# TensorE's share of a side computation moved ahead of half loads and scores in each step of an attention kernel

## The chip, the cores and the metric

The kernel runs on one core of a Trainium2 chip. The metric is the device time of one execution in microseconds (us); the time of a kernel is the median of its runs. Five engines with queues of their own take part: TensorE (PE; its weight loads are listed apart as PEld), VectorE (DVE), ScalarE (ACT), GpSimd (POOL) and SyncE (SP, which only issues DMAs).

## The reference

Two blocks follow one another. The first is attention over 8 batches, 8 heads, 576 tokens and 64 dimensions a head, in which each query keeps the 32 keys with the highest scores:

```python
scores = scale * np.matmul(q, k.transpose(0, 1, 3, 2))
kth = np.partition(scores, -top_k, axis=-1)[..., -top_k:-top_k + 1]
scores = np.where(scores >= kth, scores, -1e9)
attn = softmax(scores)          # exp of scores less their maximum, over their sum
x = np.matmul(attn, v)          # heads side by side: 576 x 512 a batch
```

The second is a mixture of depths: a gate for each token (`x @ w_gate`), and for the 128 tokens of a batch with the highest gates a two-layer network, whose result is weighted by the sigmoid of the gate and added to the row. The other rows pass through.

```python
h = np.maximum(xe @ w1, 0.0)    # 128 x 1024
out[b, top_idx] = x[b, top_idx] + g[:, None] * (h @ w2)
```

## The kernel before

**Units.** The attention is cut into 144 units of 128 query rows by two heads: 18 a batch (`per_batch`), in the order batch, tile of rows `t`, pair of heads `g`. The last tile has 64 rows and holds four heads a unit. One loop, `for n in range(-1, N)`, is a software pipeline written out by hand. Program order is kept on every engine (the class `InOrder`, whose line 45 is therefore the line of nearly every instruction in the profile), so the order of the statements is the order of each engine's queue.

**One step.** In step `n` the statements do, in this order:

- `weigh` for unit `n - 4`: TensorE turns the unit's scores (`ptr<-ident,sc`, `av<-ident,sc` for the last block) and adds a large negative number where the mask `less` says that the key isn't among the 32 (`ptr<-out_of_reach,less`). The first eight blocks need the mask's first half, the next eight its second half. Then ScalarE takes the exponentials (`pT` of the two times four blocks, `last` of the last).
- `mask_of` for unit `n - 3`: `less`, the first half by ScalarE, the second by GpSimd (by VectorE in the steps of `scatter_steps`); both need VectorE's `next`.
- `flush()`: what lies in the list `late` goes to ScalarE (the ReLU of the mixture, its copies).
- TensorE turns one or two blocks of the next batch's keys and queries into free columns of the scores' PSUM (half loads, `ps<-ident,rows`), then multiplies the scores of unit `n + 1` (`ps<-kT,qT`). ScalarE copies both out (`kT`, `qT`, `sc`).
- `values` for unit `n - 4` on TensorE: weights times values (`av<-v,pT`, 32 products, and `av<-vpair,last`, four for the last keys). It needs `pT` and `last`. ScalarE copies the result (`xs`) and, at the end of a tile, its sums (`sums`).
- VectorE: `bound_of` for unit `n` (the maxima `cand`, `best`, `bound`), between its halves what lies in `vector_late` (reciprocals `rden`, the gates' products `prod`, the mixture's counts `junk`); then `kth_of` for unit `n - 2` (`next<-y`). `flush_pool()` gives GpSimd what lies in `pool_late`.
- `what_is_below` for unit `n - 1`: ScalarE's `sides<-sc,bound`, GpSimd's `y<-sc,sides` and its short fill `y<-steps,seen`.
- the mixture's piece for step `n`, if there is one.

At the end of a batch `keep_least` adds VectorE's `low` and three reductions.

**The mixture.** `mixture` is a generator. `mix_steps` lists for each step which batch's generator is advanced by one `yield`, once or several times; the pieces of batch `b` stand in the steps of batches `b + 1` and `b + 2` (`mix_at`; a denser list for the last two mixtures, `mix_at_of`). The pieces are: the gate row through DRAM (three DMAs on SP), five counts for VectorE, the places (five small products on TensorE, advanced inside the step by `place_steps`, not by `mix_steps`), a gather of 128 rows, their four transposes (`xe_ps`), eight pieces of four products for the first layer (`h_ps`, one ReLU for every two of them) and eight of one product of 512 columns for the second (`y_ps`; the profile counts two matmuls for each). The results of TensorE's pieces lie in one PSUM bank with a single buffer (`misc`). What other engines do for a piece is put into `late`, `vector_late` or `pool_late` and goes out at the next flush.

PSUM is the reason for the tight order: the scores, the turned scores, the values and the mixture have one buffer each (`ps_sc`, `ps_tr`, `ps_av`, `ps_misc`).

Behind the loop the last units are finished statement by statement (from line 1214), and `closing` does the last batch's mixture.

Of the kernel before, what the change touches and what calls it, by code (L numbers as in the profile page):

```python
# [48 lines left out]
def kernel(  # L49
# [118 lines left out]
    def load_weights():  # L168
        sp.dma_start(
            out=wg, in_=dataclasses.replace(moe_w_gate, ap=[[0, P], [1, HD]])  # L170
        )
        sp.dma_start(out=w1, in_=moe_w1.rearrange("(c p) f -> p c f", p=P))
        sp.dma_start(out=w2, in_=moe_w2.rearrange("(c p) n -> p c n", p=P))
# [13 lines left out]
    def flush():  # L187
        while late:
            late.pop(0)()
# [15 lines left out]
    def room_for_qkv(b):  # L205

        kT = kqpool.tile([P, NHP, R + S], FP32, name="kT")  # L210
        qT = kqpool.tile([P, NHP, S], FP32, name="qT")
        return kT, qT, vbufs[b % 2]
# [98 lines left out]
    def turn_pair(rows, hp, copy=None):  # L311
        tr = ps_tr.tile([P, 2, J, P], FP32, name="ptr")
        for w in range(2):
            rows.turn(2 * hp + w, tr[:, w, :, :])
        for w in range(2):
            rows.keep(2 * hp + w, tr[:, w, :, :], copy=copy)
# [8 lines left out]
    def load_v(vb, vs):  # L325
        vt, vpair = vs
        v_rows = vb[:, JP:S, :].rearrange("h p d -> p h d")
        for hh in range(2):
            sp.dma_start(
                out=vpair[hh * R : (hh + 1) * R, :, hh, 0:D], in_=v_rows[:, hh::2, :]  # L330
            )
        for h in range(H):
            sp.dma_start(
                out=vt[:, h, :, 0:D],
                in_=vb[h, 0:JP, :].rearrange("(p j) d -> p j d", j=J),
            )

    def groups(t):

        return NHP // 2 if t == J else NHP  # L340
# [11 lines left out]
    def room_for_scores():  # L352
        return ps_sc.tile([P, 2, 2, 512], FP32, name="ps")

    def multiply(t, g, kT, qT, ps):

        n = R if t == J else P  # L360
        for u in range(2):
            for i, heads in enumerate(heads_of(t, g)):
                at = u * HALF + (0 if i else R)
                d = slice(i * D, (i + 1) * D)
                for h, r in heads:
                    pe.matmul(
                        ps[r : r + n, i, u, 0:HALF],
                        qT[d, h // 2, t * P : t * P + n],
                        kT[d, h // 2, at : at + HALF],
                    )  # L370
# [106 lines left out]
    def room_to_turn():  # L477
        return ps_tr.tile([P, 2, J, P], FP32, name="ptr"), ps_av.tile(
            [P, 512], FP32, name="av"
        )  # L480
# [62 lines left out]
    def normalise(b, t, xs):  # L543
        n = R if t == J else P
        den = sums[0:n, b * NT + t, :]
        divide(n, xs, of_batch[b][0][0:n, t, :], den)

    def keep_sums(n, xs, den):
        act.activation(den, xs[0:n, :, D], AF.Copy, bias=1e-9)
# [404 lines left out]
    def gates(b, t):  # L954
        dot_tile(t, *of_batch[b])
# [24 lines left out]
    N = len(units)  # L980
# [16 lines left out]
    mix_steps = {}  # L997
# [9 lines left out]
    for b in range(B - 1):  # L1007
        n = (b + 1) * per_batch + mix_at_of.get(b, mix_at)[6]
        mix_steps[n].remove(b)
        place_steps[n] = b  # L1010
    mixtures = {}
# [21 lines left out]
    def is_unit(n):  # L1033
        return 0 <= n < N

    def weigh(sc, tr, av, less):

        turn(sc, tr, less)
        tr_last = turn_last(sc, av, less)
        pT = ptpool.tile([P, 2, J, P], FP32, name="pT")  # L1040
        last = ptpool.tile([P, P], FP32, name="last")

        def exp():
            act.activation(pT, tr, AF.Exp, scale=scale)
            act.activation(last, tr_last, AF.Exp, scale=scale)

        return pT, last, exp
# [25 lines left out]
    def keep_least(b, bound, kth):  # L1073
        low = stats.tile([P, per_batch, 2], I32, name="low", bufs=1)
        dve.tensor_scalar(
            out=low,
            in0=bound.bitcast(I32),
            scalar1=(1 << 23) - 1,
            scalar2=1,
            op0=ALU.bitwise_and,  # L1080
            op1=ALU.bitwise_xor,
        )
        for w, of in enumerate((bound, kth, low)):
            dve.tensor_reduce(
                out=least[:, w, b : b + 1], in_=of, axis=mybir.AxisListType.XY, op=ALU.min
            )

    def mask_of(n, on=None):
        b, i = divmod(n, per_batch)
        masks[n] = mask(scs[n], next8s[b][:, i, :, :], on)  # L1090
        if i == per_batch - 1 and b < B - 1:
            keep_least(b, bounds.pop(b)[:, :, :, 7], next8s.pop(b)[:, :, :, 7])

    for n in range(-1, N):
        b, i = divmod(n, per_batch)
        if i == 0 and 0 <= b < B - 1:
            qkv[b + 1] = room_for_qkv(b + 1)
            loading = chain(
                loading, Rows(k[b + 1], q[b + 1], *qkv[b + 1][0:2]).parts()
            )  # L1100
        if 0 < n + 1 < NHP:
            turn_pair(first_rows, n + 1)
        if n == 1:
            load_v(v[0], qkv[0][2])
        if n == NHP:
            load_weights()


        gating = normalised
        if inverting is not None:  # L1110
            normalised = inverting[0:2]
            vector_late.insert(0, lambda a=inverting: normalise(*a))
            inverting = None
        else:
            normalised = None
        if gating is not None:
            vector_late.append(lambda a=gating: gates(*a))

        if is_unit(n - 4):
            tr, av = room_to_turn()
            pT, last, exp = weigh(scs.pop(n - 4), tr, av, masks.pop(n - 4))
            exp()
        if is_unit(n - 3):
            mask_of(n - 3, (act, None) if n in scatter_steps else None)
        flush()
        if is_unit(n + 1):
            b, t, g = units[n + 1]
            ps = room_for_scores()  # L1130
            kT, qT = qkv[b][0:2]
            b, i = divmod(n, per_batch)
            loads = list(islice(loading, first_loads[i] if b == 0 else loads_at[i]))
            halves = [ps[:, a, :, HALF : HALF + P] for a in range(2)]
            for load, half in zip(loads, halves):
                load[0](half)
            multiply(t, g, kT, qT, ps)
            for load, half in zip(loads, halves):
                load[1](half)
            scs[n + 1] = keep(ps, n == -1)  # L1140
        if is_unit(n - 4):
            b4, t4, g4 = units[n - 4]
            values(t4, g4, pT, last, av, qkv[b4][2])
            if n in place_steps:
                values_bank[0] = av
                next(mixtures[place_steps[n]])
            if g4 == 0:
                xs = xpool.tile([P, H, DE], FP32, name="xs")
                if t4 == 0:
                    x = xpool.tile([P, NT, HD], FP32, name="x")  # L1150
                    pg = gates_of[b4 % 2]
                    of_batch[b4] = x, pg
            keep_values(t4, g4, av, xs)
            if g4 == groups(t4) - 1:
                inverting = b4, t4, xs
                n4 = R if t4 == J else P
                keep_sums(n4, xs, sums[0:n4, b4 * NT + t4, :])
            while kept:
                kept.pop(0)()


        if is_unit(n):
            bound_of(n)
        flush_vector()
        flush_pool()
        if is_unit(n - 2):
            kth_of(n - 2)
        while after_kth:
            after_kth.pop(0)()


        if is_unit(n - 1):
            what_is_below(n - 1)

        if gating is not None:
            b, t = gating
            if t == J:
                store(out[b], of_batch[b][0])
                mixtures[b] = mixture(float(b * S), of_batch[b][1], ranks[:, b, :])
        for b in mix_steps.get(n, ()):  # L1180
            next(mixtures[b], None)
        b, i = divmod(n, per_batch)
        if i == v_at and 0 <= b < B - 1:
            load_v(v[b + 1], qkv[b + 1][2])
# [12 lines left out]
    def weigh_unit(m):  # L1197
        tr, av = other_room() if (N - m) % 2 else room_to_turn()
        weighed[m] = *weigh(scs.pop(m), tr, av, masks.pop(m)), av
# [10 lines left out]
    def sums_of(t, xs):  # L1210
        n = R if t == J else P
        keep_sums(n, xs, sums[0:n, (B - 1) * NT + t, :])

    weigh_unit(N - 4)
    weighed[N - 4][2]()
    what_is_below(N - 1)
# [188 lines left out]
```

## Time and profile before

| | |
|---|---|
| median of 3 runs | 827.2 us (826.03 to 827.62) |
| profiled execution | 828.44 us |
| its span in the profile | 826.1 us |
| instructions | 28252 |
| mean granted TensorE clock | 0.99 of full speed |
| HBM read, written | 36.93 MB, 11.55 MB |

The profile has one row for each group of instructions with the same engine, operation and tiles: busy time, mean duration, and the idle time of the engine ahead of them with what ended most of it. Its slices show the busy share in tenths in 40 equal parts of the span. The windows give the same per stretch; the waits sum up who waited for whom; the timeline lists instructions by start and duration, neighbours of one kind merged. The chain that ended last tells little here, for it consists of the last scatter alone. Matmuls are pipelined and their ends are modelled, so on TensorE distances between starts are the safer measure; a VectorE instruction is likewise shown starting some 0.08 us before the one ahead of it ends.

### The profile page before, as it was taken

Reading aid. Unit: us, or ns where it says so; the run is one execution under the profiler, and the core shown is the slowest. Engines: PE = TensorE matmul, PEld = TensorE weight load, DVE = VectorE, ACT = ScalarE, POOL = GpSimd, SP = SyncE. Lnnn points to the kernel's source line nnn. Section 1 sums busy time; section 2 is a strip of 40 time slices with the busy share of each in tenths; the row PEclk is TensorE's granted clock in tenths of the full one; section 3 lists DMA queues with packets and bytes.
Section 4 is the critical chain, followed back from the end, with each engine's and each line's share of the span. In section 5 each row is a group of like instructions: output and inputs, shape, how many; then the busy total and the mean of one; then the engine's idle time right before and its main releaser. Section 6 shows DMA issues by size and latency. Waiting matters only on the chain. (4 is left out here: it accounts for less than half of the span.)

```text
span 826.1 us, 28252 instructions
## 1 busy us (share of the span) xinstructions
PE 777.0 (94%) x10143; PEld 596.5 (72%) x10143; DVE 787.2 (95%) x4651; ACT 730.7 (88%) x1557; POOL 715.4 (87%) x722
## 2 busy tenths in 40 slices
PE   6888888888999999999999999999999999999976
PEld 5566666666887778877787777877787777767744
DVE  7899999999999999999999999999999999999960
ACT  4799999999999999999999999999999999879831
POOL 3799999999899999999899999999999998899831
PEclk9699999999999999999999999999999999999999
DMA  7931111521141221521223221512215102101021
GB/s 170 283 86 40 28 66 28 105 53 27 60 92 36 53 40 59 112 47 34 79 47 86 53 40 60 104 23 54 40 59 112 28 15 66 23 12 18 2 71 30
DMA packets 122133, 50.38 MB, mean 61 GB/s; under 512 B 116417, under 2 KB 116417, under 8 KB 120961
## 3 DMA queue, kind: packets, MB, share of 16 engines
q1 hardware_dynamic: 118672, 43.91, 22.0%
q0 software_dynamic: 1728, 4.20, 2.8%
q8 instruction: 82, 1.34, 0.8%
q14 instruction: 67, 0.54, 0.3%
q10 hardware_dynamic: 1584, 0.39, 0.2%
HBM read 36.93 MB, written 11.55 MB: 59 GB/s over the span
## 5 line engine op out<-in xcount | busy, mean ns | idle before, releaser
L45 POOL TENSOR_TENSOR y<-sc,sides 128x576 f32<-128x576 f32 x288 | 365.1, 1289 | 57.0 <-ACT sides L45 54.3
L45 DVE MAX8 cand<-sc 128x8 f32<-128x82 f32 (+1 forms) x2016 | 314.0, 228 | 2.7 <-ACT sc L45 2.7
L45 POOL TENSOR_SCALAR less<-sc,next 128x576 bf16<-128x576 f32 x135 | 232.5, 1722 | 12.9 <-DVE next L45 10.0
L45 PE MATMUL ptr<-out_of_reach,less 128*128 128x128 bf16 x1136 | 205.3, 220 | 19.5 <-POOL less L45 19.4
L45 ACT ACTIVATE sides<-sc,bound 128x576 bf16<-128x576 f32 x288 | 223.0, 787 | 0.0
L45 PE MATMUL ptr<-ident,sc 128*128 128x128 f32 x1136 | 217.0, 282 | 0.0
L45 DVE MAX8 next<-y 128x8 f32<-128x584 f32 x288 | 204.4, 751 | 1.7 <-POOL y L45 1.6
L45 PEld LDWEIGHTS av<-v,pT 128*64 128x64 f32 x4544 | 144.1, 137 | 66.9 <-ACT last L45 63.2
L45 PE MATMUL ps<-kT,qT 64*128 64x288 f32 (+1 forms) x1280 | 182.0, 431 | 5.2 <-ACT qT L45 5.2
L45 PEld LDWEIGHTS ptr<-ident,sc 128*128 128x128 f32 x1136 | 161.3, 142 | 29.1 <-issue 17.4
L45 ACT ACTIVATE pT<-ptr 128x1024 f32<-128x1024 f32 x142 | 145.3, 1023 | 33.2 <-PE ptr L45 32.2
L45 PE MATMUL av<-v,pT 128*64 128x65 f32 x4544 | 163.7, 224 | 9.3 <-ACT last L45 8.5
L45 ACT COPY sc<-ps 128x1152 f32<-128x1152 f32 (+1 forms) x144 | 162.2, 1126 | 3.5 <-PE ps L45 3.5
L45 PEld LDWEIGHTS <-less 128*128 128x128 bf16 x1296 | 136.1, 106 | 39.2 <-POOL less L45 25.2
L45 PEld LDWEIGHTS ps<-kT,qT 64*128 64x128 f32 (+1 forms) x1280 | 100.2, 178 | 41.5 <-issue 21.2
L45 ACT ACTIVATE less<-sc,next 128x576 bf16<-128x576 f32 x143 | 111.2, 777 | 12.7 <-DVE next L45 10.8
L45 DVE MATCH_REPLACE8 cand<-best,cand 128x21 f32<-128x21 f32 (+1 forms) x576 | 99.0, 180 | 0.0
L45 DVE MAX8 best<-cand 128x8 f32<-128x21 f32 (+1 forms) x576 | 90.5, 190 | 0.0
L45 PE MATMUL h_ps<-xeT,w 128*128 128x128 f32 x464 | 65.8, 286 | 0.0
L45 PEld LDWEIGHTS h_ps<-xeT,w 128*128 128x128 f32 x464 | 55.8, 191 | 9.2 <-issue 5.8
L45 PE MATMUL y_ps<-w,hT 128*128 128x512 f32 x112 | 60.6, 636 | 0.0
L45 ACT ACTIVATION_READ_ACCUMULATOR sides<-sc,bound 128x1 f32 x288 | 59.9, 208 | 0.0
(133 smaller groups left out, 866.4 us busy)
## 6 DMA issues: line engine op xcount, KB each, us to landing
v<-in_v_dram SPq DMA_DIRECT2D x64, 128.0 KB, 4.2
out_dram<-x SPq DMA_DIRECT2D x8, 1024.0 KB, 3.9
rows<-in_k_dram SPq DMA_DIRECT2D x56, 128.0 KB, 2.9
rows<-in_q_dram SPq DMA_DIRECT2D x56, 128.0 KB, 3.1
w<-in_moe_w_dram SPq DMA_DIRECT2D x2, 2048.0 KB
gate_row<-row_dram SPq DMA_DIRECT2D x7, 288.0 KB, 4.4
w<-in_k_dram SPq DMA_DIRECT2D x8, 128.0 KB, 3.2
last<-in_k_dram SPq DMA_DIRECT2D x8, 128.0 KB, 4.0
```

What stands on the lines that cost most here:

```text
L45: return lambda *a, **kw: self._tc.keep_in_program_order(fn(*a, **kw))
```

## The change

The call that advances the mixture's generators leaves the end of step `n`, where it follows `values` and everything else, and stands in step `n + 1` instead, right behind the turning and the exponentials of unit `n - 3` and ahead of the mask, the flush, the half loads and the scores. On TensorE a piece was between the products with the last keys of one step and the turning of the next; it is now between the turning and the half loads. The places, advanced by `place_steps`, stay where they were, and the pieces of the loop's last step are still issued behind the loop. The scheduled step numbers aren't changed.

```diff
+    def mix(n):
+        for b in mix_steps.get(n, ()):
+            next(mixtures[b], None)
+
     for n in range(-1, N):
...
             pT, last, exp = weigh(scs.pop(n - 4), tr, av, masks.pop(n - 4))
             exp()
+        mix(n - 1)
         if is_unit(n - 3):
             mask_of(n - 3, (act, None) if n in scatter_steps else None)
         flush()
...
                 mixtures[b] = mixture(float(b * S), of_batch[b][1], ranks[:, b, :])
-        for b in mix_steps.get(n, ()):
-            next(mixtures[b], None)
         b, i = divmod(n, per_batch)
...
+    mix(N - 1)
     weigh_unit(N - 4)
     weighed[N - 4][2]()
```

## The prediction

> **What bounds the kernel now.** I read the page first: who is busy, and when.
>
> ```profile
> PE 777.0 (94%) x10143; PEld 596.5 (72%) x10143; DVE 787.2 (95%) x4651; ACT 730.7 (88%) x1557; POOL 715.4 (87%) x722
> PE   6888888888999999999999999999999999999976
> DVE  7899999999999999999999999999999999999960
> ```
>
> Then the windows over one batch (18 steps, from the middle, where one batch repeats the last):
>
> ```profile
> core 0: us, PE busy (x) PEld busy (x) DVE busy (x) ACT busy (x) POOL busy (x), PEclk, DMA share, GB/s
> 307.00:403.10 96.10, 94.92 (x1269) 73.58 (x1266) 95.99 (x577) 91.53 (x197) 88.51 (x88) 1.00 0.27 60
> ```
>
> VectorE works 95.99 of 96.10 us: it paces the middle, at 96.1/18 = 5.34 us a step. But nobody is far behind: TensorE 94.92, ScalarE 91.5, GpSimd 88.5. The waits of the whole span say who waits for whom behind VectorE's back:
>
> ```profile
> PEld av L45 <- ACT last L45: 63.2, 132, 1.3
> POOL y L45 <- ACT sides L45: 54.3, 71, 12.0
> ACT pT L45 <- PE ptr L45: 32.2, 75, 1.6
> PEld L45 <- POOL less L45: 25.2, 30, 1.4
> ```
>
> The first and third are what the change is about: TensorE idles before `values` for ScalarE's exponentials, and ScalarE idles for the turned scores. Neither is VectorE's time.
>
> Last, the timelines of one step, engine by engine:
>
> ```profile
> 417.18 0.39 PE L45 MATMUL ps<-ident,rows 128*128 128x128 f32 x2
> 418.67 1.15 PE L45 MATMUL av<-v,pT 128*64 128x65 f32 x32
> 419.65 0.39 PE L45 MATMUL av<-vpair,last 128*64 128x130 f32 x4
> 419.98 1.16 PE L45 MATMUL h_ps<-xeT,w 128*128 128x128 f32 x8
> 420.97 0.27 PE L45 MATMUL ptr<-ident,sc 128*128 128x128 f32 x1
> ...
> 420.22 0.30 ACT L45 COPY xs<-av 128x130 f32<-128x130 f32 x1
> 420.38 0.82 ACT L45 ACTIVATE sides<-sc,bound 128x576 bf16<-128x576 f32 x1
> ```
>
> ```profile
> 414.13 1.72 POOL L45 TENSOR_SCALAR less<-sc,next 128x576 bf16<-128x576 f32 x1
> 419.49 1.71 POOL L45 TENSOR_SCALAR less<-sc,next 128x576 bf16<-128x576 f32 x1
> ...
> 421.43 2.53 POOL L45 TENSOR_TENSOR y<-sc,sides 128x576 f32<-128x576 f32 x2 [0.23 <-ACT sides L45]
> 423.91 0.22 POOL L45 TENSOR_TENSOR y<-steps,seen 128x16 f32<-128x16 f32 x1
> ```
>
> TensorE's order is turn (415.64), loads and scores (417.18), values (418.67), piece (419.98), turn (420.97). The piece costs 0.99 us from its start to the next turn's.
>
> **What the edit moves.** No instruction is added or removed. The pieces number 7 transposes of `xe`, 56 of `h` (0.99 us) and 56 of `y` (0.96), less those left in the closing. Only their place on TensorE changes: turn, piece, loads and scores, values. The queues `late`, `vector_late` and `pool_late` are flushed at the same places as before, after the new call too, so ScalarE's and GpSimd's orders stay, and so do SP's DMAs (the gate row's three follow the same stores and precede the same loads). On VectorE one `squash` goes behind a gate's product in one batch: nothing. `mix(N - 1)` behind the loop is where it was. First pieces with work on TensorE stand near 203 us.
>
> Counted from before, scores and values come after the same sum of TensorE work; the turn comes 0.99 us earlier, if its mask is there. That is the point. Take the turn at 415.64. After the change it can start at 414.65, its first half takes 0.68, but the second half needs GpSimd's `less`, which ends at 414.13 + 1.72 = 415.85. So the second half starts at about 415.91 (release 0.06) instead of 416.32, and TensorE has waited 0.58 us, time that the piece filled before. From there: second half and last block 0.86 (416.32 to 417.18), piece 0.99, loads and scores 1.49, and values start at 419.25 against 418.67: 0.58 later. Their copy `xs` on ScalarE (420.22, ready then) starts at about 420.67, 0.45 later, and with it `sides` and GpSimd's `y`. The exponentials of that unit gain nothing, for ScalarE was busy until 417.2.
>
> So the piece leaves TensorE's private order and enters a loop that closes over two steps: second half of the turn 0.86, piece 0.99, loads and scores 1.49, values 1.37, to `xs` 0.05, to `sides` 0.16, to `y` 1.05, to its fill 2.48, to `less` 0.20, `less` and release 1.78. Sum 10.43. Mean extras are 0.13 (`sums` adds 0.29 in 5 of 18 steps, second copies and double loads the rest): 10.56, or 5.28 us a step. Without the piece it was (10.56 - 0.99)/2 = 4.79. VectorE needs 5.34. The slack of the loop falls from 0.55 to 0.06 us a step: GpSimd, once late, hardly catches up.
>
> **What lateness costs.** It doesn't starve VectorE at once: `y` is ready 3.7 us before `next` reads it (424.13 and 427.82). It costs where VectorE and GpSimd collide. The gate's product and `low` take longer beside a GpSimd instruction:
>
> ```profile
> 462.08 1.12 DVE L45 CUSTOM_DVE_ANT_0 prod<-x,wg 128x512 f32<-128x512 f32 x1
> ...
> 461.91 1.73 POOL L45 TENSOR_SCALAR less<-sc,next 128x576 bf16<-128x576 f32 x1
> ```
>
> Begun 0.17 behind `less`, the product took 1.12 us; begun 0.63 behind (409.38), 0.67. So it can't move in the first 0.6 us of a `less`. Behind a `y` it waits for that one's end (57.20: 1.75 us). In a middle batch five products take 4.48 us, 1.13 above 5 x 0.67, and `low` takes 1.06 against 0.17 free (at 113.15): 2.02 us of stalls. In the first batch, where `y` is ready only 1.0 us ahead (60.27, 61.28), the products alone take 8.68: 5.33 of stalls, 3.3 more. The lost slack moves the middle towards that batch. Ends: all stalls gone, -2.02 a batch; the first batch's state everywhere, +3.3. I take +1.0, a third of the way, since `y` should keep 1 to 2.5 us of its 3.7. Over (782 - 203)/96.1 = 6.0 batches that is +6.0.
>
> The Trainium skill has a rule that speaks against any such overlap: by "SBUF — State Buffer", section "Who interferes with whom", a VectorE instruction with two SBUF inputs and a GpSimd one that reads SBUF exclude each other for the whole instruction. The rows above disagree, since the product ended 0.44 us before `less` did. By the rule it would have waited 1.56, not 0.45, and five such would add 5.5 us a batch.
>
> In the double steps near 693 to 738 us (two pieces, 1.9 us) the loop takes about 0.45 more a step; VectorE waits there 1.9 us for the gate row's DMA anyway. Ends 0 and +3 over six such steps; I take +0.5. At the end two turns lie behind double pieces: ScalarE waits 1.19 and 1.61 for them (774.22, 780.29), and VectorE later 1.35 for `y` (785.33). With the turn first that could give back 1.0; a GpSimd that arrives late takes as much. Ends -1.0 and +1.5, taken as 0.
>
> Sum: +6.5. The profiled execution took 828.4 (span 826.1 and 2.3 around it), so 834.9; it lay 1.2 above the median of the three runs, 827.2. Against the median: 833.7.
>
> **Rivals.** (1) No change: VectorE paces, the loop's 0.06 us of slack suffices, the collisions stay: 827.2 within 1.7. For it: VectorE without gaps, 3.7 us of reserve. Against: the 0.45 us shown above appears at each turn whose mask ends late.
> (2) Faster: the masks are mostly there, ScalarE's wait for `ptr` (32.2) goes, `sides` and `y` come earlier, and the products start deeper into `less`. The stalls fall by a third (-0.6 x 6.0), and the end gives 1.0: 822.6. It decides at the second half of the turn: it needs `less` to end within 0.68 us of the earlier start. In the pass above it ended 1.2 after it, in the next (turn at 419.25 + 1.31 = 420.56, mask at 421.20) 0.64 after it, just in time.
> (3) The loop becomes the bound. If a pass costs 0.3 us more than my rows (releases I can't see, the piece ahead of scores costing more), a step takes 5.43, against VectorE's 5.34; 579/5.34 = 108 steps of 0.09 and rising collisions of 1 a batch give +16: 843.
> That the edit doesn't move the work is excluded: program order is kept on each engine.
>
> **How the numbers follow.** A measurement here can tell about 0.2%, 1.7 us, from no change. Slower by collisions: 0.57, its own range 829 to 839. Rival 3: 0.20. Rival 1: 0.10. Rival 2: 0.13. Faster 0.13, same 0.10, slower 0.77. The range reaches to 826 below (leaving out most of rival 2) and 843 above (leaving out under half of rival 3).
>
> **What would show it.** Right: TensorE's wait for `last` falls under 25 us; its waits for `less` (25.2 on the weight loads) rise above 50; the five products of a middle batch take over 5.0 us in place of 4.48; VectorE still has no gaps; `y` is ready under 2.6 us before its reader. Wrong: the products unchanged or shorter (rival 1 or 2), ScalarE's wait for `ptr` near zero with earlier `y` (rival 2), or VectorE idling for `sc` or `y` in the middle (rival 3).

## The result, and the profile after

The changed kernel takes 829.2 us (median of 7 runs, 828.7 to 831.6) against 826.3 us of the kernel before in the same comparison (7 runs, 825.6 to 827.6): a ratio of 1.0037, 95% interval 1.0025 to 1.0048. It is slower by about 3.0 us, as forecast in direction; the forecast of +6.5 us was more than twice too large.

The page of the changed kernel, busy times:

```profile
PE 777.8 (94%) x10143; PEld 594.7 (72%) x10143; DVE 790.1 (96%) x4651; ACT 732.6 (89%) x1557; POOL 715.3 (87%) x722
```

VectorE works 2.9 us longer than before (787.2) with the same instructions, and still has no gaps in the middle. One middle batch in the windows of the changed kernel (columns as in the prediction):

```profile
305.18:401.85 96.67, 95.45 (x1269) 73.50 (x1265) 96.56 (x577) 91.62 (x197) 88.30 (x88) 1.00 0.27 60
```

A batch takes 96.67 us in place of 96.10, with VectorE busy for all of it. The five distances from one `low` to the next, from the second to the seventh, add up to 483.53 us where they were 480.83: +2.70 of the 3.0 us. Behind the seventh `low` the profiled executions differ by 0.2 us (135.74 and 135.54), so the double steps and the end cost next to nothing, as far as one profiled execution of each can tell. (The profiled spans, 826.7 and 826.1, differ less than the medians, because the first 50 us, where the two programs are the same, took 2.3 us more in the profiled execution of before. All comparisons of profiled executions below therefore start at a `low`.)

The waits of the changed kernel:

```profile
POOL y L45 <- ACT sides L45: 60.8, 72, 11.0
PEld L45 <- POOL less L45: 33.3, 48, 1.4
PEld av L45 <- ACT last L45: 26.1, 52, 1.2
ACT pT L45 <- PE ptr L45: 7.3, 12, 1.6
```

The edit does what it says. The wait for `last` went from 63.2 to 26.1 us and ScalarE's for `ptr` from 32.2 to 7.3: 62 us of waiting gone (16.9 came back on the weight loads as a wait with ScalarE's `less`), and the kernel is slower. Most of the 63.2 was no lost time of TensorE: it is counted on the weight loads (PEld), while the matmuls of the scores still ran. The matmuls' own wait for `last` was small, before and after:

```profile
PE av L45 <- ACT last L45: 8.5, 16, 1.1
PE av L45 <- ACT last L45: 4.1, 10, 0.7
```

What grew is GpSimd's wait for `sides`, 54.3 to 60.8, and ScalarE's wait for VectorE's `next` ahead of its half of `less`. Before and after:

```profile
ACT less L45 <- DVE next L45: 10.8, 15, 2.7
ACT less L45 <- DVE next L45: 18.8, 38, 2.5
```

In one middle batch ScalarE didn't wait for `next` at all before, and waits 1.8 us in five places after: another engine now waits for VectorE.

Where VectorE spends the 0.57 us of a batch is seen in two of its five products. The timelines of the kernel before, third product and fifth, with the `less` beside each:

```profile
344.67 0.89 DVE L45 CUSTOM_DVE_ANT_0 prod<-x,wg 128x512 f32<-128x512 f32 x1
...
344.28 1.72 POOL L45 TENSOR_SCALAR less<-sc,next 128x576 bf16<-128x576 f32 x1
...
387.83 0.83 DVE L45 CUSTOM_DVE_ANT_0 prod<-x,wg 128x512 f32<-128x512 f32 x1
...
387.37 1.72 POOL L45 TENSOR_SCALAR less<-sc,next 128x576 bf16<-128x576 f32 x1
```

and the same two of the changed kernel:

```profile
342.89 1.10 DVE L45 CUSTOM_DVE_ANT_0 prod<-x,wg 128x512 f32<-128x512 f32 x1
...
342.70 1.72 POOL L45 TENSOR_SCALAR less<-sc,next 128x576 bf16<-128x576 f32 x1
...
386.25 1.16 DVE L45 CUSTOM_DVE_ANT_0 prod<-x,wg 128x512 f32<-128x512 f32 x1
...
386.12 1.72 POOL L45 TENSOR_SCALAR less<-sc,next 128x576 bf16<-128x576 f32 x1
```

Begun 0.39 us behind `less`, the third product took 0.89 us; begun 0.19 behind, 1.10. The fifth went from 0.46 behind and 0.83 to 0.13 behind and 1.16. In all four it ends 1.28 to 1.29 us after `less` began: what GpSimd starts later, VectorE waits longer. Of the 18 steps of a batch, numbered from 0, the five products stand in steps 3, 5, 9, 13 and 17; the third and the fifth are those in 9 and 17. The first, second and fourth take 0.67, 0.99 and 1.10 us before and 0.67, 1.02 and 1.11 after. The five add up to 5.05 us, against 4.48.

### The profile page after: what moved, and what is told of

Read it like the earlier page. It is cut to its first block, busy times and chain, and to the rows that moved or that the text cites. A ratio compares the mean times of both kernels' runs of the same rounds, so it can differ in the third digit from the quotient of the medians.

```text
span 826.7 us, 28221 instructions
## 1 busy us (share of the span) xinstructions
PE 777.8 (94%) x10143; PEld 594.7 (72%) x10143; DVE 790.1 (96%) x4651; ACT 732.6 (89%) x1557; POOL 715.3 (87%) x722
## 5 line engine op out<-in xcount | busy, mean ns | idle before, releaser
L45 POOL TENSOR_TENSOR y<-sc,sides 128x576 f32<-128x576 f32 x288 | 365.5, 1290 | 63.7 <-ACT sides L45 60.8
L45 PE MATMUL ptr<-ident,sc 128*128 128x128 f32 x1136 | 225.4, 287 | 0.0
L45 PEld LDWEIGHTS av<-v,pT 128*64 128x64 f32 x4544 | 144.1, 137 | 60.4 <-ACT last L45 26.1
L45 PEld LDWEIGHTS <-less 128*128 128x128 bf16 x1296 | 140.1, 109 | 35.8 <-POOL less L45 33.3
L45 DVE MAX8 best<-cand 128x8 f32<-128x21 f32 (+1 forms) x576 | 90.3, 189 | 0.0
L45 PE MATMUL h_ps<-xeT,w 128*128 128x128 f32 x464 | 63.3, 281 | 0.0
L45 PE MATMUL y_ps<-w,hT 128*128 128x512 f32 x112 | 58.5, 617 | 0.0
L45 ACT ACTIVATION_READ_ACCUMULATOR sides<-sc,bound 128x1 f32 x288 | 57.3, 199 | 0.0
```

Source lines behind the costliest of these rows:

```text
L45: return lambda *a, **kw: self._tc.keep_in_program_order(fn(*a, **kw))
```

## The experiments

My theory, A: the 3 us are VectorE's third and fifth product, which stall longer because GpSimd's `y`, and with it its next `less`, comes later. The rivals: B, the longer loop over TensorE, ScalarE and GpSimd holds the batch by itself; C, the loss lies in the double steps and the end; and later D, that loop holds the batch at about 96.0 us in both kernels, and VectorE's stalls only fill what is left.

All kernels below are timed against the kernel before. Since most of them turned out to be about which VectorE instruction stalls, here is one table for all: the time per middle batch (mean of the two between the fourth and the sixth `low`), and how much of it VectorE spends on the four kinds of instruction that take longer beside GpSimd (distances from start to start, in us). The time of everything else on VectorE is 90.3 to 90.6 us in every row, so that the four columns account for each batch. They say where VectorE's time goes; as a stalled instruction counts as busy, they don't say which engine holds the batch.

| kernel | us, ratio (95%) | batch | prod | low | less | pick |
|---|---|---|---|---|---|---|
| before | 826.3 | 96.11 | 4.15 | 0.98 | 0.42 | 0.20 |
| changed | 829.2, 1.0037 (1.0025 to 1.0048) | 96.66 | 4.71 | 0.98 | 0.42 | 0.20 |
| e1_prod_later_before | 824.8, 0.9976 (0.9965 to 0.9988) | 96.01 | 4.70 | 0.34 | 0.42 | 0.20 |
| e1_prod_later_after | 834.7, 1.0093 (1.0075 to 1.0111) | 97.41 | 4.97 | 0.37 | 1.13 | 0.60 |
| e1_five_back | 832.1, 1.0060 (1.0041 to 1.0078) | 96.93 | 4.11 | 1.03 | 1.15 | 0.30 |
| e2_late_y_before | 831.5, 1.0060 (1.0044 to 1.0076) | 96.28 | 3.57 | 1.00 | 1.14 | 0.20 |
| e2_sides_first_before | 830.6, 1.0042 (1.0026 to 1.0057) | 96.89 | 4.99 | 0.21 | 1.14 | 0.20 |
| e2_y_only | 830.3, 1.0042 (1.0029 to 1.0055) | 96.34 | 4.36 | 0.98 | 0.42 | 0.20 |
| e3_gates_later_before | 825.1, 0.9984 (0.9972 to 0.9996) | 96.08 | 3.69 | 0.69 | 1.00 | 0.36 |
| e3_gates_later_after | 829.6, 1.0032 (1.0020 to 1.0043) | 96.09 | 3.84 | 0.98 | 0.42 | 0.49 |
| e3_behind_scores_relu | 839.1, 1.0155 (1.0142 to 1.0169) | 98.42 | 5.09 | 1.18 | 1.14 | 0.43 |
| e4_half_h_before | 824.1, 0.9974 (0.9962 to 0.9985) | 95.98 | 4.01 | 0.98 | 0.42 | 0.20 |
| e4_half_h_after | 827.5, 1.0007 (0.9995 to 1.0018) | 96.22 | 4.24 | 0.99 | 0.42 | 0.20 |
| e4_half_product_before | 822.7, 0.9954 (0.9939 to 0.9969) | 96.21 | 3.91 | 0.22 | 1.13 | 0.42 |
| e4_half_product_after | 824.4, 0.9970 (0.9958 to 0.9983) | 96.12 | 3.37 | 1.03 | 0.95 | 0.41 |

Without collisions the four would take 3.0, 0.1, 0.4 and 0.2 (from the shortest rows of each kind; `prod` 1.65 in the two e4_half_product rows, where it is shorter), 3.7 in all.

**VectorE's small work later.** Between the two halves of `cand` VectorE does its products, reciprocals, counts and, in one step a batch, a half of `less`. The edit, made on both kernels:

```diff
-            if i == 1:
-                flush_vector()
             for u in range(PARTS):
+                if i == 1 and u == 4:
+                    flush_vector()
```

Expected of the changed kernel with it: 

> The changed kernel, with VectorE's small work between the halves of cand (reciprocals, gates' products, counts) moved four maxima further down its queue (about 0.59 us). Theory A (the 3 us of the change are the third and the fifth product of a batch, which begin too early into GpSimd's less): all five products begin at least 0.7 us behind the start of less and take 0.67 us, 3.35 a middle batch in place of 5.05, the batch falls from 96.67 to about 95.0 us, the whole to 817 to 821 us. Theory B (the longer loop over TensorE, ScalarE and GpSimd holds the batch at 96.67): the products get shorter but VectorE gets gaps instead, and the time stays above 827. Theory C (the 3 us lie in the double steps and the end): the time falls as much as the kernel before does with the same edit, and the 3 us between the two stay.

Expected of the kernel before with it: 

> The kernel before, with the same shift of VectorE's small work by four maxima. Theory A: products 3.35 us a middle batch in place of 4.48, batch about 95.0 in place of 96.1, the whole 817 to 821 us, within 1 us of the changed kernel with the same shift, so that the order of TensorE no longer matters. Theory B: about 820 here, and 3 us or more below the changed kernel with the shift. Theory C: 3 us below it.

Measured: 834.7 and 824.8. Theory A's numbers failed in both. The second batch shows the intended effect (three products of 0.67 us, begun 0.74 to 1.32 behind `less`), and from then on VectorE, being faster, stands differently against GpSimd: the products meet `y` or the start of `less` instead. In the changed kernel this went further: the half of `less` that VectorE makes, and `pick`, take longer too (1.13 and 0.60 us). Yet VectorE has none of the gaps in either that theory B foresaw, so B failed as well, and the difference between the two grew from 3 to 10 us, so that theory C (the loss lies in the end) is out. What follows: the collisions aren't a fixed sum that one shift removes. They depend on where VectorE stands against GpSimd, and that moves with each change.

**Five pieces put back**, in the steps just ahead of the two products:

```diff
-        mix(n - 1)
+        if (n - 1) % per_batch not in (6, 7, 13, 14, 15):
+            mix(n - 1)
...
+        if n % per_batch in (6, 7, 13, 14, 15):
+            mix(n)
```

Expected: 

> The changed kernel, with five of a batch's 17 pieces put back to the end of their step (those of positions 6, 7, 13, 14 and 15 of 18, just ahead of the third and the fifth product), the other twelve where the change has them. Theory A: the third and fifth product take 0.89 and 0.83 us again, the batch 96.1 us, the whole 826 to 827 us. Theory B (each moved piece costs its share of the loop): 12/17 of the 3 us stay, about 828.4.

Measured: 832.1 us, slower than with all of them moved. The products did fall back (4.11 us, before 4.15), but the half of `less` on VectorE grew. It is in the timelines of this kernel:

```profile
392.44 1.22 DVE L45 TENSOR_SCALAR less<-sc,next 128x576 bf16<-128x576 f32 x1
...
390.81 2.52 POOL L45 TENSOR_TENSOR y<-sc,sides 128x576 f32<-128x576 f32 x2
```

The kernel before has this instruction with no `y` beside it:

```profile
393.33 0.50 DVE L45 TENSOR_SCALAR less<-sc,next 128x576 bf16<-128x576 f32 x1
```

In this kernel a step that goes over from the moved place to the old one holds two pieces (the moved one of the step before and its own), which I hadn't thought of: twice a batch TensorE does 0.94 us more in one step, `y` comes later (3.07 us of reserve in the median, against 3.59), and other instructions are hit. Neither theory had it.

**A part without such steps**: only the pieces of positions 10 to 17 moved. Edit: in the same way, with `(n - 1) % per_batch >= 10`. Expected: 

> Only the pieces of positions 10 to 17 (the second layer in a middle batch) have the changed place, the others the old one; no step holds two. Theory A: the third product (position 9) is 0.89 us as before, the fifth (position 17) 1.16 as after; batch 96.4, 828.0 to 829 us. If every moved piece costs its share of the 3 us: 8 of 17, 828.6, with both products grown by about half.

Measured: in a middle batch the third product is 0.89, as before, the fifth 1.05 to 1.13; batch 96.34. This is theory A's picture in the profile, product by product, and not that of an equal share for every moved piece. The time, +4.0 us by the medians with an interval of +2.4 to +4.5, is above the 1.7 to 2.7 forecast; the profiled execution is 2.1 longer from the first `low` on. Theory A holds for the batch; for the rest of the time it is inconclusive.

**`y` late, TensorE untouched.** In the kernel before, ScalarE makes `xs` twice in nine steps:

```diff
             keep_values(t4, g4, av, xs)
+            if n % per_batch in (5, 7, 8, 9, 11, 13, 14, 15, 16):
+                keep_values(t4, g4, av, xs)
```

Expected: 

> The kernel before, TensorE's order untouched; ScalarE makes the copy xs a second time (0.30 us, the same data) ahead of sides in nine of a batch's 18 steps (positions 5, 7, 8, 9, 11, 13, 14, 15 and 16), those in which the change made GpSimd's y 0.2 to 0.34 us late. Theory A (what the change costs is only the phase of GpSimd against VectorE): the third and the fifth product grow to about 1.1 us each, a middle batch to 96.5 to 96.8 us, the whole to 829 to 831 us, as the changed kernel. Theory B (what costs is the longer loop over TensorE): ScalarE has 4.5 us of idle time a batch, the copies take 2.7 of it, and the time stays at 827.

Measured: 831.5, just above theory A's range of 829 to 831, and far above theory B's 827. So the kernel gets as slow with TensorE's order untouched. But the expected picture shows in one batch of five only: the batches took 97.5, 96.15, 96.42, 96.14 and 96.72, and in the last of these the third, fourth and fifth product took 1.18, 1.15 and 1.14 us. In the batches of 96.1 the dose had been too large, and a product came ahead of `less` altogether:

```profile
367.26 0.68 DVE L45 CUSTOM_DVE_ANT_0 prod<-x,wg 128x512 f32<-128x512 f32 x1
...
367.37 2.16 POOL L45 TENSOR_SCALAR less<-sc,next 128x576 bf16<-128x576 f32 x1
```

Now the product takes 0.68 us and `less` 2.16 in place of 1.72: GpSimd pays. Lateness doesn't cost in proportion: a product that begins 0.6 us behind the start of `less` pays nothing, from there on each 0.1 us nearer costs 0.1 us, up to 0.5, and one that begins first mostly pays nothing again (but 1.40 us in e1_prod_later_before at 224.47, 0.12 ahead of `less` and 0.07 behind the start of the short fill). That the second copies act through `y` alone isn't shown: they also hold up what ScalarE does next.

**`sides` ahead of `xs`** on ScalarE, so that `y` needn't wait for values:

```diff
+            if is_unit(n - 1):
+                what_is_below(n - 1)     # sides alone; y stays where it was
             keep_values(t4, g4, av, xs)
```

Expected of the kernel before with it: 

> The kernel before, with ScalarE's sides ahead of xs and sums in each step, so that GpSimd's y no longer waits for values. Theory A: less starts when next is there, the products begin 1.0 us behind it and take 0.67 each, low some 0.2 to 0.5; VectorE's batch falls by 1.2 to 1.9 us, as far as TensorE (94.9 us busy) lets it: 95.0 to 95.4 a batch, 820 to 823 us in all. Theory B: xs and av come free 1.6 us later, TensorE waits for av, and the time is above 827.

Expected of the changed kernel with it: 

> The changed kernel with the same order on ScalarE. Theory A: the late values no longer reach y, so the products are as short as in the kernel before with this edit, and the time is within 1.5 us of it, 820 to 824 us. Theory B: the change's own loop (turn, piece, scores, values) holds the batch, and the time stays 3 us or more above the kernel before with this edit.

Measured: 830.6 and 877.1 (1.0619, 1.0602 to 1.0636). Theory A failed and B was right, in both. Values' bank now comes free some 1.5 us later (two `sides`), and TensorE's turning needs it for its last block. The changed kernel's waits with this edit:

```profile
PEld av L45 <- ACT xs L45: 78.8, 126, 0.9
PE av L45 <- ACT xs L45: 49.0, 115, 0.7
```

With the piece behind the turning there is no other work on TensorE that could cover this wait; in the kernel before the piece stands ahead of the turning and covers most of it (27.6 and 17.5 us of the same two waits there). A batch of the changed kernel takes 105.6 us here and VectorE has gaps: this is what a loop over TensorE looks like when it does become the bound, and the changed kernel alone shows none of it.

**The piece behind the scores.** First with its ReLU in the next step, as the kernel has it:

```diff
-        mix(n - 1)
...
             scs[n + 1] = keep(ps, n == -1)
+        mix(n - 1)
```

(In this first version the last step keeps the changed place, and GpSimd's adding of a piece's rows is queued together with their scaling.) Expected: 

> The pieces behind the scores, still ahead of values: turn, half loads, scores, piece, values. Scores come as early after the turn as in the kernel before, values as late as in the changed one. Theory A with the path over values, xs, sides, y and less: the products as in the changed kernel, 5.05 us a batch, 828.5 to 830 us. If the path went over the late scores and their copy sc instead: products 4.48 us, 826 to 827 us.

Measured: 895.0 us, 1.0815 (1.0789 to 1.0841). The experiment tests something else than was meant: the piece now waits for the ReLU that frees its bank, with values queued behind it.

```profile
PEld h_ps L45 <- ACT hT L45: 28.8, 20, 2.4
```

Then with that wait taken away, by a second `flush()` behind `mix(n - 1)`. Expected: 

> Pieces behind the scores and ahead of values, and ScalarE's ReLU of a piece right behind the copy sc of the same step, so that the next piece finds its PSUM bank free. Theory A, path over values, xs, sides, y and less: values are as late as in the changed kernel, the third and the fifth product about 1.1 us each, 828.5 to 831 us. If the scores' place were what costs: products as before, 826 to 827.5 us.

Measured: 839.1, well above both. This run doesn't test theory A either, since TensorE's own step got longer. From one start of `values` to the next it takes 5.49 us in the first layer's steps where it took 5.34 before and in the changed kernel, without a wait of the matmuls in those steps: from the piece's start to what follows are 1.09 us here, 0.99 before and 0.94 in the changed kernel. Sixteen pieces by 0.15 are 2.4 us, and the batch grew by 2.3 (98.42 and 96.11). TensorE's time went into the batch one for one, which theory A hadn't foreseen.

**The gates' products alone later**, by three maxima; reciprocals, counts and `less` stay:

```diff
             for u in range(PARTS):
+                if i == 1 and u == 3:
+                    while products:
+                        products.pop(0)()
...
-            vector_late.append(lambda a=gating: gates(*a))
+            products.append(lambda a=gating: gates(*a))
```

Expected of the changed kernel with it: 

> The changed kernel with the gates' products alone (not the reciprocals, counts and the mask that VectorE makes) moved three maxima, 0.44 us, down VectorE's queue. Theory A: the products begin 0.56 to 1.08 us behind the start of less, take 0.67 to 0.72 us (3.4 to 3.5 a middle batch in place of 5.05), and nothing else on VectorE or GpSimd gets longer; batch 95.1 to 95.4 us, where TensorE's own 94.9 us of work begin to bound it; 820 to 823 us. Theory B (TensorE's loop holds the batch): gaps on VectorE, 828 us or more.

Expected of the kernel before with it: 

> The kernel before with the same shift of the gates' products alone. Theory A: products 3.35 to 3.45 us a middle batch in place of 4.48, batch 95.0 to 95.3 us, 820 to 823 us, within 1.5 us of the changed kernel with the shift. Theory B: 820 to 823 here and 5 us or more below the changed kernel with the shift.

Measured: 829.6 and 825.1. In the middle the two are now alike, 96.09 and 96.08 us a batch, so the 0.57 is gone when the products begin elsewhere, with TensorE's order as changed. That is against theory B. Against theory A's size is that both stopped at 96.1, not at 95.2. The changed kernel lost most of its gain elsewhere: its second batch interval took 97.78 us in place of 96.86 (three products met `y`), and the part behind the seventh `low` 0.6 us more than before. Its ratio to before, 1.0032, can't be told from 1.0037.

This pair of runs also shows how VectorE's stalls become time. With the products moved, ScalarE hardly waits for VectorE's `next` in a middle batch (0 to 0.2 us, against 1.8 in the changed kernel), and TensorE's distances from `values` to `values` are those of the changed kernel within 0.05 us in 16 of 18 steps. The other two are 5.34 and 4.48 us in place of 5.48 and 4.92, together 0.58: the whole 0.57. The longer of the two, in the changed kernel and then with the products moved:

```profile
487.17 0.78 ACT L45 ACTIVATE less<-sc,next 128x576 bf16<-128x576 f32 x1 [0.53 <-DVE next L45]
492.62 1.15 PE L45 MATMUL av<-v,pT 128*64 128x65 f32 x32 [0.43 <-ACT last L45]
```

```profile
486.36 0.77 ACT L45 ACTIVATE less<-sc,next 128x576 bf16<-128x576 f32 x1
491.81 1.16 PE L45 MATMUL av<-v,pT 128*64 128x65 f32 x32
```

In the changed kernel ScalarE waits 0.53 us for `next`, works without a gap from there to `last`, and TensorE waits 0.43 us for that. The waits of the weight loads that grew with the order (`ps` at "issue", 26.7 to 48.3 us in all) are 7.1 us a batch in both runs, so they aren't the loss.

**Which engine holds 96.1?** First 1.35 us a batch off VectorE (five products 0.27 shorter), nothing off the others:

```diff
-            out=prod[0:n, 0:HD], in0=x, in1=wg[0:n, :],
+            out=prod[0:n, 0 : HD // 2], in0=x[:, 0 : HD // 2], in1=wg[0:n, 0 : HD // 2],
```

Expected of the kernel before with it: 

> The kernel before, the gates' products over 256 of the 512 columns (the other half of each gate is left out), which takes about 0.33 us x 5 = 1.6 us a batch off VectorE and nothing off the others. Theory A (VectorE's own work and stalls set the batch): 94.5 to 95.0 us a batch, 817 to 821 us. Theory D (the loop over TensorE, ScalarE and GpSimd sets about 96.0 and VectorE's stalls fill the rest): 95.8 to 96.1 a batch, 824 to 827 us, and VectorE's other instructions that stall beside GpSimd (low, less, pick) grow or gaps appear.

Expected of the changed kernel with it: 

> The changed kernel with the same halved products. Theory A: batch 94.9 to 95.4, 819 to 823 us, still about 0.3 to 0.6 us a batch above the kernel before with them. Theory D: 96.0 to 96.7 a batch, 826 to 829 us.

Then 0.45 us off TensorE in eight steps of a batch (1.00 to 0.55 from a piece's start to the next turning), nothing off VectorE:

```diff
-            multiply_h(ps[:, fc % 2, :], fc, xeT)
+            multiply_h(ps[:, fc % 2, :], fc, xeT, 2)     # two of four products
```

Expected of the kernel before with it: 

> The kernel before, with two of the four products in each of the mixture's first-layer pieces (half of that layer's sum is left out), 0.48 us less on TensorE in eight steps of a batch, 3.8 us a batch. Theory A: TensorE wasn't the bound, y comes earlier in those steps, the third product falls to about 0.67: batch 95.8 to 96.1, 824 to 827 us. Theory D: the batch falls by 0.5 to 1.5 us, to 94.6 to 95.6, 816 to 823 us.

Expected of the changed kernel with it: 

> The changed kernel with the same halved first-layer pieces, so that only 0.47 us instead of 0.94 stand between the turning and the loads in those eight steps. Theory A: the third product falls back to 0.67 to 0.89 us, the fifth (in the second layer's steps) stays at 1.16; batch 96.2 to 96.45, 826.5 to 828.5 us. Theory D: 95 to 96, below 825 us.

Windows of a middle batch, the columns as above; the kernel before with half products, then with half first-layer pieces:

```profile
302.60:398.50 95.90, 94.87 (x1267) 73.58 (x1267) 95.79 (x578) 91.02 (x197) 89.43 (x88) 1.00 0.26 60
```

```profile
304.79:400.78 95.99, 92.80 (x1237) 69.99 (x1233) 95.88 (x577) 90.99 (x197) 88.50 (x88) 1.00 0.28 60
```

and the changed kernel with half first-layer pieces:

```profile
402.65:498.87 96.22, 93.30 (x1237) 69.86 (x1234) 96.11 (x577) 91.34 (x197) 88.38 (x88) 1.00 0.26 60
```

In the changed kernel less TensorE work gives 0.44 us a batch: the third product falls to 0.78 (expected 0.67 to 0.89), the batch is 96.22, the time 827.5, within theory A's ranges; the fifth, expected to stay at 1.16, falls to 1.06 to 1.13. So the length of the piece that stands ahead of the loads sets how late `y` is, and that sets the stall. The two kernels with the same half pieces differ by 0.24 us a batch, as their fifth products do (1.06 and 0.82).

Less VectorE work gives the kernel before 0.2 us a batch (most batches 95.9, one 96.5) and the changed one 0.54 (96.12), not the 1.1 to 1.8 of theory A. In the kernel before `low` fell by 0.8 us as well, and nearly all of this came back as stalls on `less` (+0.7), `pick` (+0.2) and on products that now meet `y`. The batches are theory D's; the times, 822.7 and 824.4, lie between the two forecasts.

What holds the kernel before near 95.9 is TensorE. In it and in the three runs that only move or shorten its VectorE work (e1_prod_later_before, e3_gates_later_before, e4_half_product_before) the distances from `values` to `values` in a middle batch agree within 0.03 us in 17 of 18 steps (one batch of 96.5 left aside), however differently VectorE stalls; the one that differs is 5.54, 5.47, 5.52 and 5.34. They add up to 95.90 in the last of these, with two waits near `low` for ScalarE's exponentials in it (1.0 us). In none of the middle batches of the kernel before and of e4_half_product_before does ScalarE wait for VectorE's `next`. With 3.6 us of TensorE's work gone the kernel before still takes 95.98, because VectorE with its stalls takes over: ScalarE then waits 3.2 us a batch for `next`, in seven places. Two engines thus each need 95.9 to 96.0 us, and less work on one of them gives 0.1 to 0.2. Shorter work on both at once wasn't run.

**A version that beats both** is e1_prod_later_before: 824.8 us, 0.9976 (0.9965 to 0.9988). In the profiled executions 1.0 us of it lies between the second and the seventh `low` and 1.1 behind it.

## Where the prediction was right, and where it went wrong

*VectorE paces and keeps no gaps:* it has no gaps (96.56 of 96.67 us), but that isn't pacing, since its stalls count as busy. In the kernel before TensorE, with its two waits near `low`, needs 95.9 us a batch and VectorE's stalls fill what is left; in the changed kernel VectorE's `next` comes late enough for ScalarE, and through it TensorE, to wait.

*TensorE idles before `values`:* misread. The 63.2 us are of weight loads beside running matmuls; the matmuls' own wait was 8.5 us. The sign that it would fall under 25 us was just missed (26.1).

*The piece enters the loop from `less` to `y`:* right in place, and near in size for the step that the prediction followed. Counted from `low` (402.23 before, 400.96 after), that step's turning starts 0.61 us earlier (forecast 0.99), values start 0.47 later (0.58), `xs` 0.34 (0.45), GpSimd's `y` 0.31. The changed kernel's step (turning, piece, values, and GpSimd's `y`):

```profile
413.76 0.33 PE L45 MATMUL ptr<-ident,sc 128*128 128x128 f32 x1
415.44 1.11 PE L45 MATMUL h_ps<-xeT,w 128*128 128x128 f32 x8
417.87 1.15 PE L45 MATMUL av<-v,pT 128*64 128x65 f32 x32
420.47 2.52 POOL L45 TENSOR_TENSOR y<-sc,sides 128x576 f32<-128x576 f32 x2 [0.49 <-ACT sides L45]
```

*The wait for the mask at each turning, 25.2 to above 50:* wrong, 33.3. TensorE waits 0.38 and 0.39 us for it in two steps behind `low`, and is late enough from then on that the masks are there.

*The slack of the loop is used up, and `y` keeps 1 to 2.5 of its 3.7 us:* wrong. In units 36 to 125 `y` is ready 3.58 us ahead in the median and 3.39 in the mean, against 3.59 and 3.49. The lateness doesn't add up. Against VectorE, `y` of units 4 to 12 of a batch starts 0.26, 0, 0.28, 0.20, 0.22, -0.05, 0.22, 0 and 0.23 us later than before, units 13 to 15 0.3, units 0 to 3 and 16 and 17 not at all. In some steps ScalarE took back nearly all of it: in one, values come 0.57 us later against `low` and `xs` only 0.03, because `xs` had stood 0.58 us behind the end of values in the kernel before, held by `sc`, and now stands 0.05 behind. And the piece-free step near `low` starts each batch from where it was.

*+1.0 us a batch for the collisions:* the step that failed, a mis-sized term. It measured 0.57. I put it a third of the way to the first batch's state, by slack that wasn't lost. The prediction's own rows held a better way: each product stands at a known distance behind `less`, and 0.2 to 0.34 us of lateness shorten that distance one for one, down to some 0.13. That makes about +0.2 and +0.3 for the two products that stand at 0.39 and 0.46 in late steps (+0.21 and +0.33 measured), and nothing for the other three, ahead of which `y` isn't late (units 1, 3 and 11). Five intervals grew by 0.48, 0.55, 0.56, 0.55 and 0.56 us, 2.70 in all; the term had 6.0 x 1.0.

*+0.5 for the double steps, 0 for the end:* together 0.2, in one profiled execution of each.

*The rivals:* no change and faster are out by the interval. The longer loop as the bound of the changed kernel is out: with the products elsewhere the same loop runs at 96.09 us a batch. e2_sides_first_after shows what it would have looked like.

*The port rule:* the Trainium skill, "SBUF — State Buffer", section "Who interferes with whom", has whichever of a VectorE instruction with two SBUF inputs and a GpSimd one starts first hold the shared ports for its whole length. That one of the two is held, whichever comes second, agrees with the rows (1.16 us for the product, or 2.16 for `less`). "For its whole length" agrees beside `y` and not beside `less`: the product ended 0.43 us before `less` did (1.29 and 1.72 behind its start). Worked out by the rule, the two products would have gained 0.2 and 0.33 all the same, since the start of `less` moves either way.

## What to carry to other kernels

A wait of the weight loads while matmuls still run is worth nothing; look at what the reordering does to the phase of the engines that hold each other up. An engine without gaps needn't pace, since its stalls count as busy: ask whether any other engine waits for it, and whether the distances between starts on another engine stay the same when its work changes. For such a pair, write down for each instruction of the pacing engine how far behind the other's start it begins, shift that by the lateness in that very step, and read the price from rows with that distance, rather than scaling a whole state. Where two engines need nearly the same time, as TensorE and the stalled VectorE here, a saving on one of them comes back as stalls or waits: expect a fraction.

## What the runs showed of the hardware

By the profile's times a product that began 0.11 us behind the start of `less` still ran first, in 0.67 us, and `less` took 2.28 in place of 1.72 (product at 346.17, `less` at 346.06, in e2_late_y_before); another of the same kernel, also 0.11 behind (634.89 and 634.78), took 1.18 and left `less` at 1.72. Which of the two pays thus turns over within what the profile's times can tell. Behind `y` the product waits to the end of that half, and the short fill that follows pays as well (0.67 us in place of 0.22, in e1_five_back). One program had batches of 96.15 and 97.5 us side by side.
